# Query and key tiles of the plain heads: transposed in 32x32 blocks by VectorE, and five shared DRAM tiles in the second expert layer

## The chip, the cores and the metric

The kernel runs on one core of one Trainium2 chip. The metric is the device time of one execution in microseconds; several runs are taken and their median is given. The engines are called as in the profile: PE (TensorE matmul), PEld (its weight load), DVE (VectorE), ACT (ScalarE), POOL (GpSimd) and SP (SyncE, which here only issues transfers; "SPq" are its DMA instructions).

## The reference, in short

Three stages follow each other. The first is windowed attention with 4 batches, 8 heads, 576 positions and a head width of 64. Heads 0 to 3 are plain (each position sees itself and the 31 before it), heads 4 to 7 are dilated (it sees every fourth position of the last 128):

```
scores = (1 / sqrt(64)) * q @ k^T
scores = where(mask of the head, scores, -1e9)
attn   = exp(scores - max);  attn /= sum(attn) + 1e-9
x      = attn @ v                     # 2304 rows of 512
```

Then come two mixture-of-experts layers over the 2304 rows, each with 8 experts of 512 -> 1024 -> 512. The first takes the best expert of each row that a skip score lets through; the second adds a noise term to the logits and takes the best two experts.

## The kernel before, in words

**Attention.** The work is cut into 16 units of two heads of one batch. Units 0, 1, 6, 7, 10, 11, 14 and 15 hold dilated heads; units 2, 3, 4, 5, 8, 9, 12 and 13, eight in all, hold plain ones. A unit passes these steps:

- `load_qk` (L91): SP issues the transfers of q and k into the tiles `qld` and `kld`, three buffers each. A dilated tensor is one transfer (L99). A plain tensor is two, one for each head (L103), each 96 partitions x 6 x 64 floats, so 576 packets of 256 bytes.
- `qk_T` (L138), called step A: PE transposes q and k against an identity (L146), three blocks of 96 x 96 to a PSUM bank, four banks to a unit (q twice, k twice), which is 12 instructions. DVE evicts each bank: k with a copy (L158), q with a multiplication by -0.125 (L160). `qT` and `kT` exist four times.
- `scores`, step B: PE multiplies (L175), in a first part of five query blocks and a second of four. For each block DVE adds the mask and takes the minimum (L178, two instructions in the trace: the pass, and a short read of the accumulator), ACT takes the exponential and its sum (L182), DVE the reciprocal of the sum for the whole part (L184, L185, tile `rs`), and POOL multiplies (L186). The score carries a minus sign, which the factor in L160 puts in.
- `probs_T` (L197), step D: PE transposes the probabilities, ACT (L202) and DVE (L200) evict. `values` (L214, L232), step E: PE multiplies by v.

**What sets the order.** The order on PE is written out by hand: in the plan of a step (L948), A belongs to unit s + 1, B to unit s, D and E to earlier units: "A0 D0 A1 B0 A2 D1 B1 A3 X E X D2", where X is a piece of the later rows and routing work. The order on DVE, ACT, POOL and SP is chosen by a scheduler when the program is built. Right behind the last A of a unit, `ahead` issues the loads of the unit three later, once its buffers are free. The v tile comes next in SP's queue: for the first unit 13 transfers (L132).

**After attention** come the first expert layer (first matmul L741) and the second (L439 to L441). In the second layer, `put` (L1260) writes the gathered rows of an expert to a DRAM tile `xq`, `spread` (L1267) reads that tile back in four transfers, 32 partitions each, and `turn_v` (L1287) has DVE transpose the 32x32 blocks (L1294), reading with a stride and writing with a stride. There are 35 tiles `xq`, one for each expert and each of five row tiles.

Of the kernel before, what the change touches and what calls it, by code (L numbers as in the profile page):

```python
# [8 lines left out]
F32 = mybir.dt.float32  # L9
# [3 lines left out]
ALU = mybir.AluOpType  # L13
AF = mybir.ActivationFunctionType
# [4 lines left out]
BIG = 1.0e9  # L19


def dram(ap, offset, dims):
    return bass.AP(tensor=ap.tensor, offset=ap.offset + offset, ap=dims)


class Attention:
# [7 lines left out]
    def __init__(self, ctx, early, tc, bank, q, k, v, ident, xT):  # L34
        self.tc, self.nc, self.bank = tc, tc.nc, bank
        self.q, self.k, self.v = q, k, v
        self.ident, self.xT = ident, xT
        self.B, self.H, self.S, self.D = q.shape
        nc = self.nc
        self.NB = self.S // 64  # L40

        self.vp = ctx.enter_context(tc.tile_pool(name="at_v", bufs=2))
        self.wk = ctx.enter_context(tc.tile_pool(name="at_wk", bufs=2))
        fix = early.enter_context(tc.tile_pool(name="at_fix", bufs=1, side="right"))
        self.ld = early.enter_context(tc.tile_pool(name="at_ld", bufs=2, side="right"))
        NB, R = self.NB, self.S // 4


        ip = fix.tile([128, 1], I32, name="ip")
        nc.gpsimd.iota(ip, pattern=[[0, 1]], base=0, channel_multiplier=1)  # L50
        nc.vector.tensor_single_scalar(ip, ip, 63, op=ALU.bitwise_and)
        fi = fix.tile([128, 2], F32, name="fi")
        nc.vector.tensor_copy(fi[:, 0:1], ip)
        nc.vector.tensor_scalar(fi[:, 1:2], fi[:, 0:1], 32.0, None, op0=ALU.add)
        col = fix.tile([128, 96], F32, name="col")
        nc.gpsimd.iota(col, pattern=[[1, 96]], base=0, channel_multiplier=0, allow_small_or_imprecise_dtypes=True)
        inner = fix.tile([128, 96], F32, name="mask_in")
        nc.vector.tensor_scalar(inner, col, fi[:, 0:1], BIG, op0=ALU.is_le, op1=ALU.mult)
        nc.vector.tensor_scalar(col, col, fi[:, 1:2], BIG, op0=ALU.is_gt, op1=ALU.mult)
        nc.vector.tensor_max(inner, inner, col)  # L60
        first = fix.tile([128, 96], F32, name="mask_first")
        nc.vector.tensor_copy(first, inner)
        nc.vector.memset(first[:, :32], BIG)
        self.mask = [[first] + [inner] * (NB - 1), [first] + [inner] * (NB - 1)]
        rowbig = fix.tile([128, 1], F32, name="rowbig")
        for n in range(1, NB):
            for b in range(R, self.S, R):
                i0, c0 = b - 64 * n, b - 64 * n + 32
                if c0 <= 0 or i0 >= 64:
                    continue  # L70
                m = fix.tile([128, 96], F32, name=f"mask_{n}")
                nc.gpsimd.tensor_copy(m, inner)
                nc.vector.tensor_scalar(rowbig, fi[:, 0:1], float(i0), BIG, op0=ALU.is_ge, op1=ALU.mult)
                nc.vector.tensor_scalar(m[:, :min(c0, 96)], m[:, :min(c0, 96)], rowbig, None, op0=ALU.max)
                self.mask[1][n] = m
        self.kT, self.qT = [], []
        for i in range(4):
            t = fix.tile([128, 32 + self.S], F32, name=f"kT{i}")
            nc.vector.memset(t[:, :32], 0.0)
            self.kT.append(t)  # L80
            self.qT.append(fix.tile([128, self.S], F32, name=f"qT{i}"))
        self.tiles, self.vt, self.pT, self.p = {}, {}, {}, {}
# [7 lines left out]

    def load_qk(self, m):  # L91

        nc = self.nc
        b, hp, dil = self.unit(m)
        base = (b * self.H + 2 * hp) * self.S * 64
        for nm, src in (("q", self.q), ("k", self.k)):
            if dil:
                t = self.ld.tile([96, 6, 128], F32, name=f"{nm}ld", bufs=3)
                nc.sync.dma_start(t, dram(src, base, [[128, 96], [192 * 64, 6], [1, 128]]))  # L99
            else:  # L100
                t = self.ld.tile([96, 6, 2, 64], F32, name=f"{nm}ld", bufs=3)
                for h in range(2):
                    nc.sync.dma_start(t[:, :, h, :], dram(src, base + h * self.S * 64, [[64, 96], [96 * 64, 6], [1, 64]]))  # L103
                t = t.rearrange("p c h d -> p c (h d)")
            self.tiles[nm, m] = t

    def load_v(self, m):
# [30 lines left out]
    def qk_T(self, m, part):  # L138

        nc = self.nc  # L140
        b, hp, dil = self.unit(m)
        nm, g = "qk"[part // 2], part % 2
        src = self.tiles[nm, m]
        pt = self.bank("tp")[:, :288].rearrange("p (c a) -> p c a", c=3)
        for c in range(3):
            nc.tensor.transpose(pt[:, c, :], src[:, 3 * g + c, :], self.ident[:96, :96])  # L146
        t = self.kT[m % 4][:, 32:] if nm == "k" else self.qT[m % 4]
        if dil:
            o = t.rearrange("p (h s c a) -> p h s c a", h=2, s=2, c=3)[:, g]
            i_ = pt.rearrange("p c (a s) -> p s c a", s=2)  # L150
        else:
            o = t[:, 288 * g:288 * g + 288]
            i_ = pt.rearrange("p c a -> p (c a)")
        scale = 1.0 if nm == "k" else -0.125
        if m < 2 and g == 1:
            nc.scalar.activation(o, i_, AF.Copy, scale=scale)
        elif nm == "k":
            nc.vector.tensor_copy(o, i_)  # L158
        else:
            nc.vector.tensor_scalar(o, i_, scale, None, op0=ALU.mult)  # L160

    def scores(self, m, part):
        nc, NB = self.nc, self.NB
        b, hp, dil = self.unit(m)
# [11 lines left out]
                                 start=True, stop=True)  # L176
        for n in range(n0, n1):
            nc.vector.tensor_tensor_reduce(out=sm[:, n, :], in0=ps[:, n - n0, :], in1=self.mask[dil][n],  # L178
                                           scale=1.0, scalar=3.0e38, op0=ALU.add, op1=ALU.min,
                                           accum_out=nmax[:, n:n + 1])  # L180
        for n in range(n0, n1):
            nc.scalar.activation(sm[:, n, :], sm[:, n, :], AF.Exp, bias=nmax[:, n:n + 1], scale=-1.0,  # L182
# [4 lines left out]
                                in1=rs[:, n0:n1, None].to_broadcast([128, n1 - n0, 96]), op=ALU.mult)  # L187
# [332 lines left out]
def tile_attention_moe_moe(ctx, tc, q, k, v, w_skip, w_gate, w1, w2, v_gate, v_noise, noise, u1, u2, out):  # L520
    nc = tc.nc
    B, H, S, D = q.shape
    N, DM = B * S, H * D
# [30 lines left out]
    dr = ctx.enter_context(tc.tile_pool(name="dr", bufs=1, space=DRAM))  # L554
# [131 lines left out]
    for op, *t in steps:  # L686
        if t and op[0] in "hpHP":
            c = ORDER[int(t[0])]
# [265 lines left out]
    m = (128 * LT + N) // 2  # L954
    early_ = [lambda: logits_l(128 * LT, m), lambda: logits_l(m, N)] + late(rows_l, 0, 2) + [lambda: write_l(0, 256), logits_Tl]
    busy(24)
    for n in range(-LA, NU + LE):
        a, s, d, e = n + LA, n + LB, n, n - LE
        for op in plan[n].split():
            i = int(op[1]) if len(op) > 1 else 0  # L960
# [255 lines left out]
    with ExitStack() as lctx:  # L1216
# [41 lines left out]
        xT2, xq = {}, {}  # L1258

        def put(e, i):  # L1260

            if e < E:
                n = rows2[i]
                xq[e, i] = dr.tile([n, DM], F32, name=f"xq{e}_{i}")
                nc.sync.dma_start(xq[e, i], X.pop((e, i))[:n])

        def spread(e, i):  # L1267
# [418 lines left out]
```

## Time and profile before

| | |
|---|---|
| median of the runs shown | 787.04 us (787.05, 781.78, 787.04) |
| profiled execution | 781.75 us, of it 779.9 us span |
| mean granted clock of TensorE | 0.984 of full speed |
| PE busy | 738.9 us, 95% of the span |
| DVE, ACT, POOL busy | 391.0, 309.7, 267.2 us |
| first matmul of the first expert layer (L741) | 133.7 us |

How to read it: the time of an execution is its span (first to last instruction of the core) and 1.85 us around it. An engine that is busy 95% of the span is likely to carry the chain that ends last, but within attention, the first 130 us, the engines hand work to each other every microsecond, so each stretch has to be read by itself. In the rows further down, a time in front is counted from the start of the span, "x20" is a number of instructions, and what stands behind "<-" in brackets is what ended the engine's idle time. Granted clock 1.00 is the higher of TensorE's two levels.

### The profile page before, as it was taken

How to read it: one execution, taken by the hardware profiler on the slowest of the kernel's cores; microseconds unless marked ns; L12 is line 12 of the kernel's file. 1: busy time of each engine (PE TensorE's matmuls, PEld its weight loads, DVE VectorE, ACT ScalarE, POOL GpSimd, SP SyncE). 2: the span in 40 equal slices, each digit the busy share in tenths (PEclk: the TensorE clock that was granted, in tenths of full speed). 3: DMA queues.
4: the chain of work that ended last, by engine and by line, in shares of the span. 5: the costliest groups of instructions: out<-in, count | busy, mean ns of one | idle time of the engine just before them, and what ended most of it. 6: DMA issues, size and time to landing. Idle time of an engine off the chain costs nothing.

```text
span 779.9 us, 14489 instructions
## 1 busy us (share of the span) xinstructions
PE 738.9 (95%) x5428; PEld 627.5 (80%) x5428; DVE 391.0 (50%) x1242; ACT 309.7 (40%) x824; POOL 267.2 (34%) x251
## 2 busy tenths in 40 slices
PE   8999989899998999898999899999999999999994
PEld 7877768676875977787797797898997988988883
DVE  7866866728218529936644337444453552240110
ACT  5887852234225253223442433442442433332120
POOL 3322210225127133155525434523322424544011
PEclk9999989999999999999999999999999999999997
DMA  7979555597889896268898788717417445323112
GB/s 182 174 173 251 128 203 188 179 354 265 287 264 313 301 329 242 69 171 216 237 304 236 185 262 239 170 56 159 132 64 160 121 139 92 115 29 46 15 25 29
DMA packets 133420, 138.54 MB, mean 178 GB/s; under 512 B 45184, under 2 KB 85248, under 8 KB 133344
## 3 DMA queue, kind: packets, MB, share of 16 engines
q1 hardware_dynamic: 122224, 113.39, 47.1%
q0 software_dynamic: 9808, 22.86, 14.8%
q10 hardware_dynamic: 1312, 1.31, 0.5%
q8 instruction: 44, 0.72, 0.4%
q14 instruction: 32, 0.26, 0.1%
HBM read 105.22 MB, written 32.31 MB: 176 GB/s over the span
## 4 chain that ended last, share of the span: by engine, by line
PE 65%; DMA 11%; DVE 10%; issue 5%; ACT 4%; POOL 3%; SPq 1%; POOLq 0%; DVEq 0%; ACTq 0%
PE pt L439 8%; PE pt L441 8%; PE pt L440 8%; PE pt L749 5%; PE s L741 4%; DMA xg<-xs,gidx 4%; PE s L439 3%; PE po L441 3%; PE s L440 3%; PE s L441 3%; PE po L439 3%; PE po L440 3%; ACT sm L182 3%; DMA xq<-xg 3%; PE s L175 2%
## 5 line engine op out<-in xcount | busy, mean ns | idle before, releaser
L434 POOL TENSOR_TENSOR wlo<-wraw,whi 128x512 fp32r<-128x512 f32 x76 | 109.7, 1500 | 145.0 <-ACT whi L433 120.6
L439 PE MATMUL pt<-whi,hh 128*128 128x512 f32 (+1 forms) x320 | 127.7, 399 | 3.9 <-ACT y L1450 3.9
L440 PE MATMUL pt<-wlo,hh 128*128 128x512 f32 (+1 forms) x320 | 126.6, 396 | 0.0
L441 PE MATMUL pt<-whi,hl 128*128 128x512 f32 (+1 forms) x320 | 126.6, 396 | 0.0
L434 DVE TENSOR_TENSOR wlo<-wraw,whi 128x512 fp32r<-128x512 f32 x84 | 83.9, 1010 | 85.1 <-ACT whi L433 78.3
L433 ACT ACTIVATE whi<-wraw 128x512 fp32r<-128x512 f32 x160 | 91.1, 622 | 56.9 <-PE po L440 17.1
L1210 POOL DMA_INDIRECT out_dram<-y,sidx x40 | 63.0, 1575 | 123.1 <-ACT y L1450 120.4
L713 POOL DMA_INDIRECT xg<-xs,gidx x51 | 51.1, 1002 | 132.1 <-DMA xq<-xg 45.3
L439 PEld LDWEIGHTS pt<-whi,hh 128*128 128x128 f32 (+1 forms) x320 | 58.7, 184 | 20.2 <-ACT y L1450 5.2
L439 PE MATMUL s<-xh,whi 128*128 128x256 f32 (+1 forms) x256 | 72.5, 283 | 1.3 <-DVE hl L1436 1.3
L441 PE MATMUL s<-xh,wlo 128*128 128x256 f32 (+1 forms) x256 | 72.5, 283 | 0.0
L441 PE MATMUL po<-xh,wlo 128*128 128x352 f32 x224 | 72.5, 324 | 0.0
L439 PE MATMUL po<-xh,whi 128*128 128x352 f32 x224 | 72.5, 324 | 0.0
L440 PE MATMUL s<-xl,whi 128*128 128x256 f32 (+1 forms) x256 | 72.4, 283 | 0.0
L440 PE MATMUL po<-xl,whi 128*128 128x352 f32 x224 | 72.2, 322 | 0.0
L441 PEld LDWEIGHTS pt<-whi,hl 128*128 128x128 f32 (+1 forms) x320 | 58.8, 184 | 15.9
L440 PEld LDWEIGHTS pt<-wlo,hh 128*128 128x128 f32 (+1 forms) x320 | 58.9, 184 | 15.3 <-issue 0.2
L1436 DVE SCALAR_TENSOR_TENSOR hl<-po,hh 128x352 fp32r<-128x352 f32 x56 | 29.2, 522 | 71.1 <-ACT hh L1435 69.4
L1450 ACT ACTIVATE y<-pt,slots 128x512 f32<-128x512 f32 (+1 forms) x40 | 27.3, 682 | 88.0 <-PE pt L441 68.0
L182 ACT ACTIVATE sm<-sm,nmax 128x96 f32<-128x96 f32 x144 | 51.9, 362 | 18.6 <-DVE nmax L178 18.2
L1436 DVE SCALAR_TENSOR_TENSOR hl<-s,hh 128x256 fp32r<-128x256 f32 (+1 forms) x64 | 27.3, 427 | 57.2 <-ACT hh L1435 52.5
L186 POOL TENSOR_TENSOR sm<-sm,rs 128x480 f32<-128x480 f32 (+1 forms) x32 | 29.1, 910 | 78.3 <-DVE nmax L178 52.2
(407 smaller groups left out, 1468.8 us busy)
## 6 DMA issues: line engine op xcount, KB each, us to landing
wraw<-in_moe_w_dram SPq DMA_DIRECT2D x40, 1024.0 KB
whi<-in_moe_w_dram SPq DMA_DIRECT2D x12, 1024.0 KB
wlo<-in_moe_w_dram SPq DMA_DIRECT2D x12, 1024.0 KB
xq<-xg SPq DMA_DIRECT2D x28, 256.0 KB
xs<-xq SPq DMA_DIRECT2D x112, 64.0 KB
out_dram<-zt SPq DMA_DIRECT2D x46, 128.0 KB
xs<-xr SPq DMA_DIRECT2D x13, 256.0 KB
v<-in_v_dram SPq DMA_DIRECT2D x7, 432.0 KB
```

Of the source, the lines that this page charges most:

```text
L182: nc.scalar.activation(sm[:, n, :], sm[:, n, :], AF.Exp, bias=nmax[:, n:n + 1], scale=-1.0, accum_out=ssum[:, n:n + 1])
L186: nc.gpsimd.tensor_tensor(out=sm[:, n0:n1, :], in0=sm[:, n0:n1, :], in1=rs[:, n0:n1, None].to_broadcast([128, n1 - n0, 96]), op=ALU.mult)
L433: nc.scalar.activation(hi, src, AF.Copy)
L434: (eng or nc.vector).tensor_tensor(out=lo, in0=src, in1=hi.bitcast(F32), op=ALU.subtract)
L439: nc.tensor.matmul(out, lhsT=a[0], rhs=b[0], start=start, stop=False)
L440: nc.tensor.matmul(out, lhsT=a[0], rhs=b[1], start=False, stop=False)
L441: nc.tensor.matmul(out, lhsT=a[1], rhs=b[0], start=False, stop=stop)
L713: gather.last = nc.gpsimd.indirect_dma_start(out=xg, out_offset=None, in_=xs[:n, :], in_offset=bass.IndirectOffsetOnAxis(ap=idx, axis=0))
L741: nc.tensor.matmul(ph[:, 128 * f:128 * f + 128], lhsT=w[:, c, 128 * f:128 * f + 128], rhs=self.x[:, c], start=c == 0, stop=c == KC - 1)
L749: nc.tensor.matmul(self.py, lhsT=self.h[:, 4 * g + f], rhs=w[:, f], start=g == 0 and f == 0, stop=g == 1 and f == 3)
L1210: s = nc.gpsimd.indirect_dma_start(out=out, out_offset=bass.IndirectOffsetOnAxis(ap=idx, axis=0), in_=y, in_offset=None, compute_op=ALU.add)
L1436: nc.vector.scalar_tensor_tensor(hl[1][:, f, s_], in0=ph, scalar=0.0, in1=hl[0][:, f, s_].bitcast(F32), op0=ALU.max, op1=ALU.subtract)
```

## The change

For plain units `load_qk` brings q and k in as [128, 576]: four transfers to a tensor instead of two, each 32 partitions x 18 x 32 floats, so 576 packets of 128 bytes each. Partition 32h + a then holds, for half a head h, row a of each group of 32 positions. `qk_T` makes the whole transposed tensor of a plain unit with one DVE instruction that transposes 32x32 blocks (128 x 576), without PE and PSUM. Dilated units are transposed by PE as before. The factor -0.125 moves from the eviction into the masked minimum (its `scale` operand), and the masks are multiplied by -8 to match. The 35 DRAM tiles `xq` of the second layer become five, one for each row tile, that the experts use in turn. Lines behind the edit shift by one or two: scores L174, minimum L177, exponential L181, reciprocal L183 and L184, transposing probabilities L196.

```diff
     def load_qk(self, m):
         for nm, src in (("q", self.q), ("k", self.k)):
+            t = self.ld.tile([128, 768], F32, name=f"{nm}ld", bufs=3)
             if dil:
-                t = self.ld.tile([96, 6, 128], F32, name=f"{nm}ld", bufs=3)
+                t = t[:96].rearrange("p (c d) -> p c d", c=6)
                 nc.sync.dma_start(t, dram(src, base, [[128, 96], [192 * 64, 6], [1, 128]]))
             else:
-                t = self.ld.tile([96, 6, 2, 64], F32, name=f"{nm}ld", bufs=3)
-                for h in range(2):
-                    nc.sync.dma_start(t[:, :, h, :], dram(src, base + h * self.S * 64, [[64, 96], [96 * 64, 6], [1, 64]]))
-                t = t.rearrange("p c h d -> p c (h d)")
+                t = t[:, :576].rearrange("p (g d) -> p g d", d=32)
+                for h in range(4):
+                    nc.sync.dma_start(t[32 * h:32 * h + 32], dram(src, base + (h // 2) * self.S * 64 + (h % 2) * 32,
+                                                                  [[64, 32], [32 * 64, self.S // 32], [1, 32]]))
...
     def qk_T(self, m, part):
+        t = self.kT[m % 4][:, 32:] if nm == "k" else self.qT[m % 4]
+        if not dil:
+            if g == 0:
+                nc.vector.transpose(out=t, in_=src.rearrange("p g d -> p (g d)"))
+            return
...
-        scale = 1.0 if nm == "k" else -0.125
...
-            nc.vector.tensor_scalar(o, i_, scale, None, op0=ALU.mult)
...
     def scores(self, m, part):
-                                           scale=1.0, scalar=3.0e38, op0=ALU.add, op1=ALU.min,
+                                           scale=-0.125, scalar=3.0e38, op0=ALU.add, op1=ALU.min,
...
         def put(e, i):
-                xq[e, i] = dr.tile([n, DM], F32, name=f"xq{e}_{i}")
+                xq[e, i] = dr.tile([n, DM], F32, name=f"xq{i}")
```

How the order moves, at the place where unit 4 follows unit 3. Unit 4 has the tiles `kT_192` and `qT_194`, unit 5 `kT_195` and `qT_197`; the row with `mask_first` is the first minimum of unit 4. On DVE before, the last reciprocal of unit 3 stands among the q evictions of unit 5:

```order
L158 COPY kT_192<-tp 128x288
L160 TENSOR_SCALAR qT_197<-tp 128x288
L184 TENSOR_SCALAR rs<-ssum 128x4
L160 TENSOR_SCALAR qT_197<-tp 128x288
L185 RECIPROCAL rs<-rs 128x4
L178 ISA sm,nmax<-s,mask_first 128x96
```

On DVE of the changed kernel:

```order
L183 TENSOR_SCALAR rs<-ssum 128x4
L184 RECIPROCAL rs<-rs 128x4
L149 STREAM_TRANSPOSE qT_194<-qld 128x576
L149 STREAM_TRANSPOSE kT_192<-kld 128x576
L177 ISA sm,nmax<-s,mask_first 128x96
```

Before, what stands behind the reciprocal's first half makes a tile of unit 5; now both transposes behind the reciprocal make the tiles of unit 4 itself, whose scores the next row reads.

On PE, the scores of unit 4, before:

```order
L146 MATMUL tp<-ident,qld 128x96 x3
L197 MATMUL pt<-ident,sm 96x128 x3
L146 MATMUL tp<-ident,qld 128x96 x3
L175 MATMUL s<-kT_192,qT_194 64x96 x10
L146 MATMUL tp<-ident,kld 128x96 x3
L197 MATMUL pt<-ident,sm 96x128 x3
L175 MATMUL s<-kT_192,qT_194 64x96 x8
L146 MATMUL tp<-ident,kld 128x96 x3
```

and in the changed kernel:

```order
L231 MATMUL po_613<-pT,v_391 64x64
L196 MATMUL pt<-ident,sm 96x128 x6
L174 MATMUL s<-kT_192,qT_194 64x96 x10
L196 MATMUL pt<-ident,sm 96x128 x3
L174 MATMUL s<-kT_192,qT_194 64x96 x8
L231 MATMUL po_714<-pT,v_391 64x64
```

The four groups of L146, which made unit 5's tiles, are gone from around the scores; what is left of PE's order is as it was. At units 3 and 5 the DVE rows stand in the same way; at units 2, 8, 9 and 12 one of the two transposes stands behind the last sum (L183) of the unit ahead and the other earlier, at unit 13 both stand behind it.

## Rows read from the trace of the kernel before

**Rows 1.** Windows of 20 us in attention: busy time (and count) of each engine
```profile
core 0: us, PE busy (x) PEld busy (x) DVE busy (x) ACT busy (x) POOL busy (x), PEclk, DMA share, GB/s
20.00:40.00 20.00, 19.38 (x326) 16.65 (x326) 15.79 (x103) 18.28 (x84) 7.06 (x9) 1.00 0.87 167
60.00:80.00 20.00, 18.20 (x291) 14.19 (x290) 12.87 (x80) 14.87 (x61) 4.53 (x7) 1.00 0.94 232
```

**Rows 2.** Timeline of PE: first scores of units 2 to 5, 8, 12, 13
```profile
18.39 1.04 PE L175 MATMUL s<-kT,qT 64*64 64x96 f32 x20
...
23.30 1.04 PE L175 MATMUL s<-kT,qT 64*64 64x96 f32 x20
...
26.20 1.39 PE L232 MATMUL po<-pT,v 96*64 96x64 f32 x40
...
28.81 1.04 PE L175 MATMUL s<-kT,qT 64*64 64x96 f32 x20
...
34.32 1.04 PE L175 MATMUL s<-kT,qT 64*64 64x96 f32 x20
...
46.98 1.04 PE L175 MATMUL s<-kT,qT 64*64 64x96 f32 x20
54.06 1.04 PE L175 MATMUL s<-kT,qT 64*64 64x96 f32 x20
...
75.79 1.04 PE L175 MATMUL s<-kT,qT 64*64 64x96 f32 x20
82.92 1.04 PE L175 MATMUL s<-kT,qT 64*64 64x96 f32 x20
89.66 1.04 PE L175 MATMUL s<-kT,qT 64*64 64x96 f32 x20
```

**Rows 3.** Chain of waits from 28 to 36 us: start, duration, what
```profile
29.85 0.40 PE tp L146 x3
...
34.14 0.25 PE tp L146 x3
```

**Rows 4.** Timeline of ACT: exponentials, first and last of unit 4, first of 5
```profile
30.31 0.38 ACT L182 ACTIVATE sm<-sm,nmax 128x96 f32<-128x96 f32 x1
...
33.34 0.36 ACT L182 ACTIVATE sm<-sm,nmax 128x96 f32<-128x96 f32 x1
...
36.04 0.37 ACT L182 ACTIVATE sm<-sm,nmax 128x96 f32<-128x96 f32 x1 [0.45 <-DVE nmax L178]
```

**Rows 5.** Timeline of DVE between unit 4 and unit 5
```profile
34.14 0.18 DVE L185 RECIPROCAL rs<-rs 128x4 f32<-128x4 f32 x1
34.24 0.79 DVE L160 TENSOR_SCALAR qT<-tp 128x288 f32<-128x288 f32 x2
35.52 0.26 DVE L178 CUSTOM_DVE_ANT_0 sm<-s,mask_first 128x96 f32<-128x96 f32 x1 [0.49 <-PE s L175]
```

**Rows 6.** Groups by line, shapes apart, DVE: count, busy us, mean ns
```profile
L1294 DVE STREAM_TRANSPOSE xt<-xs 128x512 f32<-128x512 f32 x28 | 30.8, 1098 | 21.9 <-DMA xs<-xq 21.2
...
L160 DVE TENSOR_SCALAR qT<-tp 128x288 f32<-128x288 f32 x30 | 13.3, 451 | 10.2 <-PE tp L146 9.7
...
L812 DVE COPY xr<-tp 128x512 f32<-128x512 f32 x9 | 6.2, 684 | 1.3 <-PE tp L807 1.3
...
L1294 DVE STREAM_TRANSPOSE xt<-xs 128x384 f32<-128x384 f32 x7 | 6.0, 863 | 5.2 <-DMA xs<-xq 5.0
```

**Rows 7.** Tile qld: issues on SP, ns min/median/max; then timeline of SP
```profile
L103 SPq DMA_DIRECT2D qld<-in_q_dram x16: 384/508/2976, 2.8 to 64.3; - x16
...
13.52 7.07 SPq L132 DMA_DIRECT2D v<-in_v_dram x13
```

**Rows 8.** Transfers in 7 to 9 us (256-byte packets), in 25 to 28 us (32-byte)
```profile
DMA packets 2131, 0.53 MB, mean 266 GB/s; under 512 B 2131, under 2 KB 2131, under 8 KB 2131
...
DMA packets 3508, 0.11 MB, mean 36 GB/s; under 512 B 3508, under 2 KB 3508, under 8 KB 3508
```

**Rows 9.** Windows of 5 us (columns as in the first group)
```profile
100.00:105.00 5.00, 4.21 (x65) 3.69 (x65) 4.74 (x34) 2.65 (x13) 0.46 (x1) 0.75 0.37 104
105.00:110.00 5.00, 5.00 (x42) 4.20 (x38) 1.74 (x12) 2.91 (x12) 1.36 (x2) 0.57 0.34 97
```

More of the change, by code (lines that the diff above doesn't have):

```diff
@@ L57, in __init__ @@
         inner = fix.tile([128, 96], F32, name="mask_in")
-        nc.vector.tensor_scalar(inner, col, fi[:, 0:1], BIG, op0=ALU.is_le, op1=ALU.mult)
-        nc.vector.tensor_scalar(col, col, fi[:, 1:2], BIG, op0=ALU.is_gt, op1=ALU.mult)
-        nc.vector.tensor_max(inner, inner, col)
+        nc.vector.tensor_scalar(inner, col, fi[:, 0:1], -8 * BIG, op0=ALU.is_le, op1=ALU.mult)
+        nc.vector.tensor_scalar(col, col, fi[:, 1:2], -8 * BIG, op0=ALU.is_gt, op1=ALU.mult)
+        nc.vector.tensor_tensor(out=inner, in0=inner, in1=col, op=ALU.min)
         first = fix.tile([128, 96], F32, name="mask_first")
         nc.vector.tensor_copy(first, inner)
-        nc.vector.memset(first[:, :32], BIG)
+        nc.vector.memset(first[:, :32], -8 * BIG)
         self.mask = [[first] + [inner] * (NB - 1), [first] + [inner] * (NB - 1)]
@@ L72, in __init__ @@
                 nc.gpsimd.tensor_copy(m, inner)
-                nc.vector.tensor_scalar(rowbig, fi[:, 0:1], float(i0), BIG, op0=ALU.is_ge, op1=ALU.mult)
-                nc.vector.tensor_scalar(m[:, :min(c0, 96)], m[:, :min(c0, 96)], rowbig, None, op0=ALU.max)
+                nc.vector.tensor_scalar(rowbig, fi[:, 0:1], float(i0), -8 * BIG, op0=ALU.is_ge, op1=ALU.mult)
+                nc.vector.tensor_scalar(m[:, :min(c0, 96)], m[:, :min(c0, 96)], rowbig, None, op0=ALU.min)
                 self.mask[1][n] = m
@@ L146, in qk_T @@
             nc.tensor.transpose(pt[:, c, :], src[:, 3 * g + c, :], self.ident[:96, :96])
[L147 to L150, printed above, removed]
-        else:
-            o = t[:, 288 * g:288 * g + 288]
-            i_ = pt.rearrange("p c a -> p (c a)")
-        scale = 1.0 if nm == "k" else -0.125
-        if m < 2 and g == 1:
-            nc.scalar.activation(o, i_, AF.Copy, scale=scale)
-        elif nm == "k":
+        o = t.rearrange("p (h s c a) -> p h s c a", h=2, s=2, c=3)[:, g]
+        i_ = pt.rearrange("p c (a s) -> p s c a", s=2)
+        if m < 2 and g == 1:
+            nc.scalar.activation(o, i_, AF.Copy)
+        else:
             nc.vector.tensor_copy(o, i_)
-        else:
-            nc.vector.tensor_scalar(o, i_, scale, None, op0=ALU.mult)
     def scores(self, m, part):
```

## The prediction, made before the changed kernel ran

> **What bounds the kernel now.** I read the busy times by window first, then the chain of waits in the stretch that the edit touches, then the timelines of the engines on that chain. In the windows of attention the reader is to see that PE is busy 19.38 of 20 us from 20 to 40 us, with ACT at 18.28 and DVE at 15.79, all at full granted clock [rows 1]: PE sets the pace, and ACT is close behind. The chain of waits from 28 to 36 us agrees: it stays on PE, and between the scores of unit 4 and those of unit 5 it holds four groups of the transposes that the change removes, two of 0.40 us and two of 0.25 us, 1.30 us together [rows 3]. From first scores to first scores, unit 2 to 3 takes 4.91 us, 3 to 4 takes 5.51, 4 to 5 takes 5.51 [rows 2]. The timelines of ACT and DVE show the second loop, nearly as long: scores of unit 4 start at 28.81, its first exponential at 30.31, its last at 33.34, ending 33.70; the last reciprocal follows at 34.14, and DVE is free for the next thing at 34.24 [rows 2, 4, 5]. Before, PE does not wait for this loop: unit 5's scores start at 34.32, because its tiles were made a unit earlier, and DVE's first minimum waits for PE until 35.52 [rows 2, 5].
>
> **The change, part by part.**
>
> *Removed on PE.* 1.30 us on the chain for each plain unit, eight of them: 10.4 us if PE stayed the bound everywhere. That is the most the change can give.
>
> *Removed on DVE.* Four evictions of 0.45 us [rows 6] a unit; two run in 0.79 us [rows 5], so some 1.6 us. The multiplication by -0.125 costs nothing where it went: the minimum is the same pass with another constant. The masks are built once, by as many instructions.
>
> *Added on DVE.* Two transposes of 128 x 576. The trace has the same operation at 128 x 512 in 1.098 us and at 128 x 384 in 0.863 us, thus 1.84 ns a column [rows 6]; at 576 that gives 1.22 us, the upper end, since those read and write with strides. The lower end is a plain pass: 0.684 us for 512 columns and 0.451 for 288, thus 1.04 ns a column and 0.75 us for 576 [rows 6]. The new ones are contiguous on both sides, like the plain passes, so I take d = 0.8 us and keep both ends. [...]
>
> *Moved on DVE, and the wait that it adds.* This is the step that decides. The rows of the order show both transposes of units 3, 4 and 5 behind the last reciprocal of the unit ahead, and PE's scores need them. So PE now waits for the second loop. Unit 5's scores would start at 34.24 + 2d + 0.1 for the hand-over (an estimate: 34.24 less the 34.14 of the step before it), that is at 34.34 + 2d instead of 34.32 [rows 2, 5]. From scores to scores this is 28.81 to 34.34 + 2d, 5.53 + 2d; the k evictions no longer stand among the minima, which can take back 0.15 us, since nine exponentials at 0.36 us are 3.24 us and ran in 3.39 [rows 4]. With d = 0.8 a period is 7.0 us. Behind the waiting scores on PE stand the next probability transposes and values, which are late with them, and ACT waits for the scores through the minimum. Three such periods are 21.0 us in place of 15.93 (18.39 to 34.32 [rows 2]): +5.1 us. The PE relief there buys nothing; PE is simply idle while DVE transposes.
>
> *Unit 2* has one transpose in that place: 5.4 + 0.8 = 6.2 us. Against the 4.91 and 5.51 us of the units behind it [rows 2] this is 0.7 to 1.3 more, and the unit ahead of it, whose period held unit 2's PE transposes, can be up to 1.30 us shorter [rows 3]. Between -0.6 and +1.3 I take +0.5.
>
> *Units 8, 9, 12, 13.* Here X pieces lengthen the periods: unit 7 to 8 takes 7.08 us, 12 from 11 takes 7.13, 13 from 12 takes 6.74 [rows 2]. PE alone could save 1.30 in each. One transpose in the loop gives 6.2 us, which is below 7.1, so units 8 and 12 may gain 0.9 each and 9 a little; two, at unit 13, give 7.0, a loss of 0.3. That is -1.8 at best; PE is busy 18.20 of 20 us there and DVE also carries row work [rows 1], so I take -1 and keep -1.8 to 0.
>
> *Loads.* 32 more transfers, each 0.51 us of SP by the median [rows 7]: 16 us of SP in all. Twelve of them come ahead of the first v, whose 13 issues begin at 13.52 and take 7.07 us [rows 7]; 6 us later they would end near 26.6, where PE multiplies by v at 26.20 [rows 2]. I take +1 us for that (0 to 2). In packets, the first three plain units have 6,912 of 256 bytes, at 2131 in 2 us [rows 8] 6.5 us; now 13,824 of 128 bytes: 13.0 us at the same price each, or 11.8 us at the pace of the 32-byte packets, 3508 in 3 us [rows 8]. The transposes come almost a unit later than the PE ones did, so most of this is hidden; it is cover that would be gone in the second rival.
>
> *Shared xq tiles.* A put must wait until the spread of the expert before has read its tile. The names of SP's waits and the order of its rows in the second layer are as before, and the puts stand behind those reads on the same queue. Nothing.
>
> *Sum.* 5.1 + 0.5 - 1 + 1 = 5.6, say +5.5 us at the end of attention. What follows is PE's chain with the same order, so it passes through. Against the profiled execution: 781.75 + 5.5 = 787.3 us. That execution lies with the lower of the three runs; two of three are 5.3 us higher, and I assume the changed kernel has the same two levels: 787.04 + 5.5 = **792.5, say 792 us**. With d at its ends the four places (two transposes at units 3, 4, 5 and 13) move the sum by -0.4 and +3.4.
>
> **The rivals.**
>
> *The relief of PE wins.* If the transposes are cheap or the exponentials end early enough, units stay bound by PE, and 1.30 us goes from each of eight: -10.4 us, 776.6 us; -5 if half do. For it: PE is 97% busy from 20 to 40 us. Against it: the order on DVE, and ACT at 18.28 of 20 [rows 1]. It decides from a period below 5.5 us, which needs 2d near 0.
>
> *Loads late and transposes slow.* With d = 1.22 the sum is +9. If the loads also reach the transposes late, early units wait for the queue: 13.0 us less 6.5 is 6.5 us at most for the first three, and I count half. Together +9 to +13: 796 to 800 us. For it: SP and the queues are busy from the start, DMA share 0.87 [rows 1]. It decides once a 128-byte packet costs as much as one of 256. [...]
>
> *The clock falls in the new waits.* From 100 to 105 us PE is busy 4.21 of 5 us with DVE at 4.74, and the granted clock is 0.75, in the next 5 us 0.57, between its two levels [rows 9]; ten us of PE work at that mean of 0.66 lose 3.4 us. New idle of 1.6 us a unit from 20 to 45 us can bring one such fall there: 792.5 + 3.4 = 796 us. If instead the new order avoids the old fall, 789 us.
>
> **How the numbers follow.** A measurement of this kernel can tell about 1%, 7.9 us, from no change: below 779.2 is faster, above 794.9 slower. Chances: the forecast, +1 to +7.9 us, 0.45; loads and slow transposes 0.24; the clock 0.12; the relief of PE 0.19, nearly all of it below 779. So faster 0.17, same 0.46, slower 0.37. The range: low end 778, where most of the relief comes, high end 804, the second rival with one clock fall; the forecast's own range is 786 to 797 by the two levels of the runs and the ends of d.
>
> **What would show it.** In the changed profile: transposes near 0.8 us (1.2 would mean the upper end); from 20 to 45 us PE's busy time falls by 2 to 4 us in 20 and its scores wait for DVE's transposes at units 3, 4 and 5; those periods are near 7.0 us; the first matmul of the expert layer stands near 139 us instead of 133.7; the rest of the program keeps its length. The prediction is wrong if the periods stay at 5.5 us or below, if the scores wait for loads and not for transposes that have started, or if the later units give back more than 2 us.

## The result, and the profile after

Twenty runs of each kernel give a median of 787.10 us (781.63 to 789.88) after the change and 783.47 us (776.28 to 788.44) before it. The ratio of the runs is **1.0063, 95% interval 1.0042 to 1.0084**: slower by 4.9 us of 783.47. The two medians by themselves lie 3.6 us apart, a ratio of 1.0046, inside the interval. So the change is slower, clear of noise, by less than 1%. The profiled execution after has a span of 784.6 us against 779.9, and the first matmul of the first expert layer stands at 139.84 us against 133.56 (timeline of PE; the table ahead has 133.7, from the chain of waits).

The window of 20 to 40 us (columns as in [rows 1]) shows where to look:

```profile
20.00:40.00 20.00, 13.87 (x195) 11.15 (x193) 12.55 (x75) 14.14 (x63) 5.76 (x7) 0.81 0.60 115
60.00:80.00 20.00, 18.95 (x301) 15.20 (x301) 14.71 (x80) 15.91 (x68) 5.62 (x7) 1.00 0.74 168
```

PE lost 5.5 us of busy time in the first of them, more than the work that left it (nine groups of three transposes, at most 0.47 us each, 4 us), and no other engine took its place as a busy one: from 20 to 40 us the core waits. The timeline of PE, which answers to [rows 2], says for what. These are the first scores of units 2 to 6 and, between them, the first transposes of the dilated unit 6:

```profile
18.24 1.87 PE L174 MATMUL s<-kT,qT 64*64 64x96 f32 x20 [3.82 <-DVE rs L184]
26.27 1.04 PE L174 MATMUL s<-kT,qT 64*64 64x96 f32 x20 [2.44 <-DVE kT L149]
33.19 1.04 PE L174 MATMUL s<-kT,qT 64*64 64x96 f32 x20 [1.00 <-DVE kT L149]
39.98 0.47 PE L153 MATMUL tp<-ident,qld 96*128 96x96 f32 x3 [2.69 <-DMA qld<-in_q_dram]
40.95 1.62 PE L174 MATMUL s<-kT,qT 64*64 64x96 f32 x20
47.90 1.04 PE L174 MATMUL s<-kT,qT 64*64 64x96 f32 x20
```

Before, PE waited for nothing at these scores. Now those of units 3 and 4 wait for the k transpose, and ahead of unit 5's PE stands for 2.69 us before a load. Unit 2's wait for DVE too, for 3.82 us, and yet start no later than before (18.24 against 18.39), with no transposes to do on PE ahead of them. The periods are 8.03, 6.92 and 7.76 us (forecast 7.0 each, before 4.91, 5.51, 5.51). The timeline of DVE at the start of unit 4, which answers to [rows 5], is the gap as forecast:

```profile
31.52 0.18 DVE L184 RECIPROCAL rs<-rs 128x4 f32<-128x4 f32 x1
31.70 0.78 DVE L149 STREAM_TRANSPOSE qT<-qld 128x576 f32<-128x576 f32 x1
32.40 0.73 DVE L149 STREAM_TRANSPOSE kT<-kld 128x576 f32<-128x576 f32 x1
...
34.39 0.26 DVE L177 CUSTOM_DVE_ANT_0 sm<-s,mask_first 128x96 f32<-128x96 f32 x1 [1.25 <-PE s L174]
```

Last reciprocal, two transposes, then DVE itself waits 1.25 us for the scores that waited for it. One transpose takes 0.78 us and the next starts 0.70 us after it; the group has 8 for q and 8 for k (by line, DVE, as in [rows 6]):

```profile
L149 DVE STREAM_TRANSPOSE qT<-qld 128x576 f32<-128x576 f32 x8 | 6.2, 778 | 0.4 <-issue 0.4
L149 DVE STREAM_TRANSPOSE kT<-kld 128x576 f32<-128x576 f32 x8 | 6.1, 762 | 0.4 <-DMA v<-in_v_dram 0.4
```

The timeline of SP, which answers to [rows 7], shows the second thing, the issues of v for the first unit at 19.10 instead of 13.52, and unit 5's q behind them at 26.26 (before: 20.70):

```profile
17.00 2.06 SPq L105 DMA_DIRECT2D kld<-in_k_dram  x4
19.10 7.05 SPq L134 DMA_DIRECT2D v<-in_v_dram  x13
26.26 3.16 SPq L105 DMA_DIRECT2D qld<-in_q_dram  x4
```

A third thing is the clock. By windows of the changed kernel, the column before the last two is the granted clock:

```profile
18.00:24.00 6.00, 5.59 (x45) 4.34 (x45) 2.57 (x23) 3.17 (x17) 1.28 (x2) 0.50 0.60 127
...
28.00:32.00 4.00, 4.00 (x62) 3.65 (x60) 2.51 (x18) 3.90 (x20) 1.14 (x2) 0.62 0.59 95
32.00:40.00 8.00, 4.32 (x85) 3.38 (x83) 5.11 (x27) 5.71 (x24) 2.80 (x4) 1.00 0.70 112
40.00:45.00 5.00, 5.00 (x51) 4.19 (x51) 3.25 (x15) 2.39 (x11) 0.00 (x0) 0.66 1.20 237
```

After PE had stood still for 3.82 us ahead of 18.24 the granted clock is 0.50, the lower level, for 6 us, where it had been 1.00 before the change.

So the profile after holds three suspects for the same 20 us: transposes in the gap, loads that come late, and the clock. The trace alone can't part them, since an engine's idle time is put down to whichever came last.

### The profile page after: what moved, and what is told of

Read it like the earlier page. It is cut to its first block, busy times and chain, and to the rows that moved or that the text cites. A ratio compares the mean times of both kernels' runs of the same rounds, so it can differ in the third digit from the quotient of the medians.

```text
span 784.6 us, 14333 instructions
## 1 busy us (share of the span) xinstructions
PE 735.6 (94%) x5332; PEld 622.6 (79%) x5332; DVE 393.0 (50%) x1226; ACT 308.6 (39%) x824; POOL 268.0 (34%) x251
## 2 busy tenths in 40 slices
DMA packets 152364, 138.54 MB, mean 177 GB/s; under 512 B 64128, under 2 KB 104192, under 8 KB 152288
## 4 chain that ended last, share of the span: by engine, by line
PE 66%; DMA 13%; DVE 8%; ACT 4%; issue 3%; SPq 3%; POOL 2%; POOLq 0%; DVEq 0%; ACTq 0%
PE pt L438 9%; PE pt L440 8%; PE pt L439 8%; PE s L740 5%; PE po L440 4%; PE po L438 4%; PE po L439 4%; PE s L438 4%; PE s L439 4%; PE s L440 4%; PE pt L748 4%; ACT sm L181 2%; DMA xg<-xs,gidx 2%; PE s L174 2%; DMA qld<-in_q_dram 2%
## 5 line engine op out<-in xcount | busy, mean ns | idle before, releaser
L433 DVE TENSOR_TENSOR wlo<-wraw,whi 128x512 fp32r<-128x512 f32 x84 | 85.6, 1030 | 89.3 <-ACT whi L432 79.7
L440 PEld LDWEIGHTS pt<-whi,hl 128*128 128x128 f32 (+1 forms) x320 | 59.0, 184 | 15.9
L181 ACT ACTIVATE sm<-sm,nmax 128x96 f32<-128x96 f32 x144 | 51.8, 361 | 23.9 <-DVE nmax L177 23.7
```

The source lines that it names most:

```text
L433: (eng or nc.vector).tensor_tensor(out=lo, in0=src, in1=hi.bitcast(F32), op=ALU.subtract)
L440: nc.tensor.matmul(out, lhsT=a[1], rhs=b[0], start=False, stop=stop)
```

## The experiments

In all tables and sentences, "k on POOL" means that POOL instead of SP issues the k loads of plain units. The first scores of the units and the start of the expert layer come from each kernel's one profiled execution, the ratio from 6 or 12 runs against runs of the kernel before (20 of each for the change itself; early2_cheap ran once):

| kernel | scores of unit 2 | 3 | 4 | 5 | 6 | expert layer | ratio to before (95%) |
|---|---|---|---|---|---|---|---|
| before | 18.39 | 23.30 | 28.81 | 34.32 | 39.71 | 133.56 | 1 |
| the change | 18.24 | 26.27 | 33.19 | 40.95 | 47.90 | 139.84 | 1.0063 (1.0042 to 1.0084) |
| xq_only | 17.94 | 22.84 | 28.35 | 33.86 | 39.26 | 133.04 | 0.9998 (0.9970 to 1.0025) |
| loads128 | 18.02 | 22.92 | 32.30 | 40.10 | 45.49 | 140.15 | 1.0066 (1.0042 to 1.0091) |
| early2 | 17.18 | 23.78 | 32.45 | 41.97 | 48.17 | 139.16 | 1.0028 (0.9997 to 1.0059) |
| cheap_late | 19.81 | 27.70 | 35.56 | 42.84 | 48.23 | 132.22 | not comparable |
| early2_cheap | 19.27 | 23.29 | 28.99 | 34.51 | 39.90 | 125.13 | not comparable |
| late_pool | 14.68 | 23.39 | 31.42 | 38.52 | 45.47 | 134.65 | 0.9950 (0.9916 to 0.9984) |
| early2_pool | 14.64 | 20.62 | 26.03 | 32.41 | 38.91 | 131.03 | 0.9940 (0.9910 to 0.9969) |
| before_pool | 17.86 | 22.91 | 28.42 | 33.93 | 39.32 | 126.13 | 0.9898 (0.9858 to 0.9939) |
| dbl | 20.59 | 29.19 | 37.78 | 46.55 | 53.48 | 150.44 | 1.0206 (1.0158 to 1.0255) |
| clock | 18.46 | 25.78 | 32.42 | 40.00 | 45.39 | 135.46 | 1.0060 (1.0033 to 1.0087) |
| mixed_early2 | 16.59 | 21.49 | 27.01 | 32.52 | 38.03 | 130.77 | 0.9960 (0.9925 to 0.9995) |
| mixed_pool | 18.26 | 23.29 | 28.81 | 34.32 | 39.71 | 130.34 | 0.9969 (0.9935 to 1.0003) |

The theory at the start was the one of the prediction, the gap; the first rival was that the loads cost, the second that the clock does.

**The shared tiles alone (xq_only).** Before, with one line of the change:

```diff
-                xq[e, i] = dr.tile([n, DM], F32, name=f"xq{e}_{i}")
+                xq[e, i] = dr.tile([n, DM], F32, name=f"xq{i}")
```

> The kernel before with one part of the change alone: the five shared DRAM tiles of the second layer, attention untouched. Theory (the cost of the change comes from the transposes that wait in the gap between two units): no difference, a ratio to before of 1.000 within 0.002. Rival (the shared tiles add a wait between the write of one expert's rows and the reads of the expert before): up to the whole 1.006.

Measured 0.9998, no difference within some 2 us. So the cost is looked for in attention.

**The loads alone (loads128).** Before, with four transfers of 128-byte packets, still transposed by PE:

```diff
-                    nc.sync.dma_start(t[:, :, h, :], dram(src, base + h * self.S * 64, [[64, 96], [96 * 64, 6], [1, 64]]))
+                    for j in (0, 32):
+                        nc.sync.dma_start(t[:, :, h, j:j + 32], dram(src, base + h * self.S * 64 + j, [[64, 96], [96 * 64, 6], [1, 32]]))
```

> The kernel before with the loads of the plain units cut as in the change: four transfers to a tensor, 576 packets of 128 bytes each, but still 96 partitions and transposed by PE. Theory (gap): the loads alone cost 0 to 2 us, ratio 1.000 to 1.003, since PE then waits for some of them at units 3 to 5 only. Rival (the loads are the price: twice the issues on SP and twice the packets): 1.006 or more, with PE waiting for qld and kld by 5 us or more in the first 45 us.

Measured 1.0066: as much as the whole change, and the theory's 0 to 2 us is missed. The rival holds by its ratio, though the waits below sum to 3.6 us and not to 5. Every wait of PE for a transfer from 17 to 49 us in its timeline, with first scores of units 3 to 5 among them:

```profile
22.92 1.04 PE L176 MATMUL s<-kT,qT 64*64 64x96 f32 x20
27.51 0.31 PE L233 MATMUL po<-pT,v 96*64 96x64 f32 x4 [0.79 <-DMA v<-in_v_dram]
28.41 0.91 PE L233 MATMUL po<-pT,v 96*64 96x64 f32 x22 [0.59 <-DMA v<-in_v_dram]
30.54 0.71 PE L147 MATMUL tp<-ident,qld 96*128 96x96 f32 x3 [0.76 <-DMA qld<-in_q_dram]
32.30 1.68 PE L176 MATMUL s<-kT,qT 64*64 64x96 f32 x20
39.15 0.44 PE L147 MATMUL tp<-ident,qld 96*128 96x96 f32 x3 [1.47 <-DMA qld<-in_q_dram]
40.10 1.04 PE L176 MATMUL s<-kT,qT 64*64 64x96 f32 x20
```

The reader sees v first, then the loads behind v in SP's queue. In this kernel SP begins v at 19.21, in the change at 19.10: the delay is that of 12 more issues at about 0.5 us. These transfers to 96 partitions are as late as those to 32 partitions in the change, and cost as much (1.0066 against 1.0063); a transfer to 32 partitions by itself was not tried.

**The order alone (early2).** The change, with the last reciprocal of a unit, and the sum ahead of it, held behind both transposes of the next:

```diff
...
+        with self.tc.issue_after(self.turned[m + 1]) if part and m + 1 in self.turned else nullcontext():
-        nc.vector.tensor_scalar(rs[:, n0:n1], ssum[:, n0:n1], 1.0e-9, None, op0=ALU.add)
+            nc.vector.tensor_scalar(rs[:, n0:n1], ssum[:, n0:n1], 1.0e-9, None, op0=ALU.add)
```

> The changed kernel with one edit of DVE's order: the second reciprocal of a unit must stand behind both transposes of the next plain unit, so that these run while ACT still takes the last four exponentials. Theory (gap): the periods from scores to scores at units 3, 4, 5 fall from 8.0, 6.9 and 7.8 us to about 6.0 and the ratio to before goes from 1.006 to 0.997 to 1.001 (4 to 7 us less than the changed kernel). Rival (late loads): the transposes wait for their data in the new place, periods stay near 7 us, ratio 1.004 to 1.008. Rival (clock): the granted clock below 1.00 goes only if the waits go.

Measured 1.0028, between the ranges of the theory and of the rival; its interval overlaps the change's. Unit 6 starts at 48.17, no earlier than in the change: at units 4 and 5 the gap is empty, at unit 3 a wait of 1.02 us is left, and the time is gone all the same. DVE makes unit 4's tiles by 28.92, and then (timeline of DVE, then of PE)

```profile
27.49 0.78 DVE L149 STREAM_TRANSPOSE qT<-qld 128x576 f32<-128x576 f32 x1
28.19 0.73 DVE L149 STREAM_TRANSPOSE kT<-kld 128x576 f32<-128x576 f32 x1
...
34.12 0.26 DVE L177 CUSTOM_DVE_ANT_0 sm<-s,mask_first 128x96 f32<-128x96 f32 x1 [4.92 <-PE s L174]
```

```profile
28.21 0.34 PE L232 MATMUL po<-pT,v 96*64 96x64 f32 x4 [1.62 <-DMA v<-in_v_dram]
29.00 0.31 PE L232 MATMUL po<-pT,v 96*64 96x64 f32 x4 [0.45 <-DMA v<-in_v_dram]
29.74 1.33 PE L232 MATMUL po<-pT,v 96*64 96x64 f32 x22 [0.44 <-DMA v<-in_v_dram]
32.45 1.50 PE L174 MATMUL s<-kT,qT 64*64 64x96 f32 x20
40.20 0.72 PE L153 MATMUL tp<-ident,qld 96*128 96x96 f32 x3 [3.19 <-DMA qld<-in_q_dram]
```

PE waits 2.5 us in the middle of the values for v and 3.19 us for unit 6's q. In the change the first is not there and the second is 2.69 us: the gap had already made PE late. The theory of one chain falls; a theory of two chains side by side takes its place.

**Cheap loads, first with the transposes in the gap, then without (cheap_late, early2_cheap).** Two kernels that compute attention on shuffled positions: q and k of a plain unit come as one contiguous transfer to a tensor. Other rows are routed behind it, so only the time to the expert layer counts.

```diff
-                for h in range(4):
-                    nc.sync.dma_start(t[32 * h:32 * h + 32], dram(...))
+                nc.sync.dma_start(t.rearrange("p g d -> p (g d)"), dram(src, base, [[576, 128], [1, 576]]))
```

The first of them also queues the transposes of units 3, 4, 5 and 13 behind the last reciprocal of the unit ahead, the second has the edit of the kernel above.

> The changed kernel with q and k of plain units brought in by one contiguous transfer to a tensor (128 packets of 2304 bytes), which puts the numbers in another arrangement, so that attention is computed on shuffled positions; the transposes of units 3, 4, 5 and 13 are held behind the last reciprocal of the unit ahead, as in the changed kernel. Theory (gap): periods at units 3 to 5 stay at 6.9 us or above, ratio 1.003 to 1.006; the late load of unit 6 goes (2.7 us of PE idle, of which some 0.3 us count). Rival (late loads): 1.000 or below.

> Both suspects taken away: the contiguous loads that shuffle positions, and the second reciprocal held behind the transposes. Only the time up to the first matmul of the expert layer counts, since other rows are routed behind it. Theory (two chains): periods at units 3 to 5 of 5.0 to 6.0 us and a start of the expert layer at 125 to 130 us, against 133.6 before, 139.8 in the change and 132.2 with cheap loads and transposes in the gap. Rival (only the loads cost): about 132. Rival (only the gap costs): about the same as the order alone gave with the real loads, 139.

In the first, units 3 to 5 keep periods of 7.89, 7.86 and 7.28 us (from the scores of unit 2 at 19.81 to those of unit 5 at 42.84), so the gap costs by itself; yet the expert layer starts at 132.22. In the second the periods are 4.02, 5.70, 5.52 and the expert layer starts at 125.13. Neither part alone gives that: with the order alone (early2) it starts at 139.16.

**k on POOL (early2_pool, late_pool).** One word in the loads of the change, with the order of the kernel above and, in the second kernel, with the transposes held in the gap:

```diff
-                    nc.sync.dma_start(t[32 * h:32 * h + 32], dram(...))
+                    (nc.gpsimd if nm == 'k' else nc.sync).dma_start(t[32 * h:32 * h + 32], dram(...))
```

This word does two things. POOL issues the k loads, and their packets come out larger: the kernel moves the same 138.54 MB with 18,432 fewer packets under 512 bytes, as many as the k loads of plain units have in the change, and 1,024 more from there to 8 KB. The packets of the whole kernel (from the pages) are, in the change, in early2_pool and in the kernel before:

```profile
DMA packets 152364, 138.54 MB, mean 177 GB/s; under 512 B 64128, under 2 KB 104192, under 8 KB 152288
DMA packets 134956, 138.54 MB, mean 180 GB/s; under 512 B 45696, under 2 KB 86272, under 8 KB 134880
DMA packets 133420, 138.54 MB, mean 178 GB/s; under 512 B 45184, under 2 KB 85248, under 8 KB 133344
```

With k on POOL the small packets are nearly as few as before the change (45,696 under 512 bytes against 45,184). So these kernels take away late loads, but don't tell fewer issues on SP from fewer packets, as the rival in the first of the two expectations here asks.

> The reordered changed kernel with the k loads of plain units issued by POOL, so that SP has as many issues as before the change and the data is the right one. Theory (two chains): the waits for v at 27 to 30 us and for unit 6's qld at 40 us go, ratio 0.992 to 0.999. Rival (packets, not issues, are what is late): the waits stay, ratio 1.002 to 1.006. Rival (POOL's issues hold up its own multiplications): the second transposes of probabilities are late, ratio above 1.003.

> The changed kernel with the k loads of plain units issued by POOL (right data, SP relieved), but the transposes of units 3, 4, 5 and 13 held behind the last reciprocal of the unit ahead, as in the changed kernel. Theory (the gap costs by itself): periods at units 3 to 5 stay at 6.9 us or more, ratio 1.003 to 1.007. Rival (the late loads are the whole cost): as the other kernel with k on POOL, 0.994.

With both cures the ratio is 0.9940, inside the theory's range, and no scores from 17 to 40 us wait:

```profile
20.62 1.04 PE L174 MATMUL s<-kT,qT 64*64 64x96 f32 x20
26.03 1.04 PE L174 MATMUL s<-kT,qT 64*64 64x96 f32 x20
32.41 1.04 PE L174 MATMUL s<-kT,qT 64*64 64x96 f32 x20
38.91 1.04 PE L174 MATMUL s<-kT,qT 64*64 64x96 f32 x20
```

With the gap put back and the loads relieved:

```profile
23.39 1.86 PE L179 MATMUL s<-kT,qT 64*64 64x96 f32 x20 [3.45 <-DVE kT L152]
31.42 1.04 PE L179 MATMUL s<-kT,qT 64*64 64x96 f32 x20 [1.38 <-DVE kT L152]
38.52 1.80 PE L179 MATMUL s<-kT,qT 64*64 64x96 f32 x20 [2.18 <-DVE kT L152]
```

Both start unit 2 at 14.6 to 14.7 and unit 6 at 38.91 and 45.47: **the gap by itself is 6.6 us at unit 6**, 6.1 of them between the scores of units 2 and 5 (23.84 us against 17.77). At the expert layer 3.6 of it are left, and in the runs the two can't be told apart (0.9940, 0.9950): the expectation of 1.003 to 1.007 is missed, and its rival, 0.994, lies inside the interval. So the gap's cost is shown in the profiles, and not in the time of the whole. Whether the scheduler would close the gap without the edit once the loads are on POOL, no run here shows; that moving the loads changes the order that it gives DVE is seen in the control, which follows.

**The control: k on POOL in the kernel before (before_pool).** The same word, in the loads of the kernel before.

> A control: the kernel before with the k loads of plain units issued by POOL, transposes on PE as they were. Theory (SP had slack before, the gain of the last kernel with k on POOL comes from the transposes that left PE): ratio 0.998 to 1.002. Rival (the gain is SP's relief alone): 0.993 to 0.996.

0.9898, the best of the kernels that can be compared, and beyond both expectations. So the gain of 0.9940 above is not the transposes'. Little of it comes from the first 45 us (unit 6 at 39.32 against 39.71): 1.7 us are there at unit 14 (95.98 against 97.70), 6.1 at unit 15 and 7.4 at the expert layer, so most of it comes at 100 us. In the kernel before, DVE had put pieces of routing ahead of the q evictions of unit 15, and the granted clock fell behind the wait of 2.05 us, to 0.75 and 0.57 in windows of 5 us [rows 9]:

```profile
100.80 0.47 PE L146 MATMUL tp<-ident,kld 96*128 96x96 f32 x3 [2.05 <-DVE qT L160]
```

In the control the scheduler puts these evictions ahead of much of the routing, PE doesn't wait for them, and the same windows read

```profile
100.00:105.00 5.00, 4.82 (x85) 4.00 (x83) 5.00 (x22) 3.47 (x13) 1.84 (x2) 1.00 0.43 118
105.00:110.00 5.00, 4.45 (x73) 3.34 (x70) 4.46 (x33) 4.41 (x21) 0.99 (x1) 1.00 0.57 175
```

Unit 15's scores start at 101.44 instead of 107.54, and the expert layer at 126.13 instead of 133.56. This cause is read from the two traces; no run moved the evictions alone.

**Transposes twice (dbl).**

```diff
+                for _ in range(2):
-                nc.vector.transpose(out=t, in_=src.rearrange("p g d -> p (g d)"))
+                    nc.vector.transpose(out=t, in_=src.rearrange("p g d -> p (g d)"))
```

> The changed kernel with each of the 16 transposes done twice (0.70 us more each). Theory (gap chain alone sets the pace at units 3, 4, 5 and 13): two more transposes in each of four gaps, 5.6 us, and part of 0.7 at units 2, 8, 9 and 12: ratio to before 1.013 to 1.017. Theory (late loads run beside it, nearly as long): at unit 5 and behind it part is hidden, ratio 1.009 to 1.013. Rival (only the loads cost): 1.006 to 1.008.

1.0206, above all the ranges: 11.2 us more than the change, if the ratios are taken times 783.47, with some 4 us of uncertainty either way. Sixteen transposes of 0.70 us are 11.2 us, but by the profiles not all of them count. The expert layer starts 10.6 us later than in the change, and 1.0 of that is there at the first scores of unit 0 already (8.88 against 7.84). From the scores of unit 2 to those of unit 5 six more transposes, 4.2 us, add 3.3 (25.96 against 22.71); in this kernel the scheduler puts one q transpose of units 3 and 4 ahead of the last sum. From unit 6 to the expert layer 5.0 of 5.6 us arrive, so those that were forecast to be half hidden mostly count. At unit 5 no wait for a load is left (timeline of PE), the gap has taken its place:

```profile
46.55 1.04 PE L175 MATMUL s<-kT,qT 64*64 64x96 f32 x20 [3.85 <-DVE kT L150]
```

**The clock (clock).** The change, with small matmuls that nobody reads where PE waits ahead of units 2 to 5:

```diff
+    for s_, k in ((2, 28), (3, 16), (4, 8)):
+        plan[s_ - LB] = plan[s_ - LB].replace("B0", f"Y{k} B0")
+    plan[5 - LB] = "Y16 " + plan[5 - LB]
```

> The changed kernel with small matmuls that nobody reads (28, 16, 8 and 16 of 128 columns, some 0.1 us each) where PE waits ahead of the scores of units 2 to 5. Theory (the clock that fell in the new waits is part of the price): the granted clock stays at 1.00 from 16 to 45 us, unit 3's period falls from 8.0 to about 7.0 us and unit 5's from 7.8 to 7.2, ratio 1.003 to 1.005. Rival (the slow stretches lie beside the two chains and cost nothing): ratio 1.006. Rival (the fillers run into the scores): 1.008 or more.

The clock mostly holds (windows of this kernel; the change had 0.50, 0.62 and 0.66):

```profile
18.00:24.00 6.00, 5.51 (x61) 4.51 (x61) 2.97 (x24) 3.66 (x19) 1.77 (x2) 0.72 0.50 121
...
28.00:32.00 4.00, 2.64 (x58) 2.37 (x54) 2.71 (x15) 4.00 (x18) 1.82 (x2) 1.00 0.79 121
...
40.00:45.00 5.00, 5.00 (x91) 4.40 (x91) 3.75 (x26) 3.56 (x17) 0.96 (x1) 1.00 1.31 232
```

In the profile unit 6 comes 2.5 us earlier than in the change and the expert layer 4.4 us, but the ratio is 1.0060, the same as the change's. In that profile one price can be seen: from unit 5 to unit 6 it is 5.39 us with the granted clock at 1.00, as before the change, and 6.95 in the change, at 0.66. What the fallen clock costs the whole is not settled; in the runs the fillers gave nothing back, as the first rival said.

**The change where PE is the bound (mixed_early2, mixed_pool).** Units 2 to 5 as before, units 8, 9, 12 and 13 by DVE, first with all loads on SP, then with k on POOL:

```diff
...
-        if not dil:
+        if not dil and m >= 6:
             if g == 0:
...
```

> The change for units 8, 9, 12 and 13 only, with the second reciprocal of the unit ahead held behind their transposes; units 2 to 5 load and transpose as in the kernel before. Theory (two chains of nearly equal length in the first 45 us, the transposes in the gap and the late loads; later units have slack on SP and are bound by PE): the early periods stay at 4.9, 5.5 and 5.5 us, each of the four later units gets up to 1.3 us shorter, ratio 0.995 to 0.999. Rival (late loads at any place): PE waits for qld or v between 45 and 90 us, ratio 1.000 to 1.004.

> Transposes by DVE for units 8, 9, 12 and 13 only, and the k loads of all plain units issued by POOL. Theory (the transposes by DVE give something where PE is the bound, units 8 to 13, and cost where ACT's loop is): ratio to before 0.984 to 0.989, below the 0.990 of the control with k on POOL and all transposes on PE. Rival (the gain of these kernels is the order that the scheduler makes when it takes the loads to be early, and the transposes by DVE give nothing): 0.990 to 0.994.

0.9960 and 0.9969: the first lies in the theory's range, the second above both of its ranges. But in the first the four units give nothing: from the scores of unit 6 to those of unit 13 it takes 50.1 us against 50.0 before, and 1.7 us are there at unit 6 already, where units 2 to 5 still load and transpose as before. With k on POOL the same stretch takes 48.6 us against 49.1 in the control, half a microsecond less, while the ratio of the control (0.9898) is the better one; the two intervals overlap only at 0.9935 to 0.9939. So no kernel here shows, in its runs, a gain that the transposes by DVE would bring over the same loads with PE.

## Why the prediction was right, and which step was not

*The direction and the size.* Forecast +5.5 us, a ratio of 1.007 on the 787.04 us shown; 792 stands to that as 1.0063. Measured 1.0063. That the time itself, 787.10, lies 4.9 us below 792 is mostly the base: the runs shown then had two levels by chance, and twenty runs spread from 776 to 788 with the median 3.6 us lower; the rest is that the medians rose by 3.6 us and not by 5. The assumption of two levels was wrong.

*The duration.* Taken 0.8, measured 0.778 and 0.762, and 0.70 from start to start. The contiguous form is thus near the 0.75 us estimated from the plain pass for 576 columns [rows 6]; with one shape the trace can't part the pace from a fixed cost. The strided form of the second layer took 1.098 us for fewer columns [rows 6]. The nearest row was the plain pass, not the row with the same name. The minimum with `mask_first` took 0.253 us with the factor in it, 0.255 before (by line, mean of 16 each).

*The wait.* Scores wait for the transposes at units 3 and 4 as forecast. At unit 5 two things end almost together: PE stands before unit 6's q until 39.98, DVE's second transpose ends at 40.64, and the scores start at 40.95. The three periods are 22.7 us together, forecast 21.0, before 15.9. So the step held in kind. PE's busy time from 20 to 40 us fell by 5.5 us, not by the 2 to 4 forecast.

*The step that failed* is the one on the loads: "6 us later they would end near 26.6 ... I take +1 us for that". Alone they cost 1.0066, as much as the whole change. SP's 12 more issues were counted and the delay of v was right to half a microsecond (forecast 6, measured 5.6); what was missed is how many things stand behind v on the same queue: unit 5's q and k, and then unit 6's, for which PE waits in its fixed order (0.76 and 1.47 us with the loads alone, 2.69 in the change).

*The sum* added the two. They lie side by side. Four kernels with the transposes on DVE cross them, by the start of unit 6: neither 38.91 (early2_pool), the gap alone 45.47 (late_pool), the loads alone 48.17 (early2), both 47.90 (the change). Alone they cost 6.6 and 9.3 us, together 9.0. (Some of the 9.3 is lost ahead of unit 2, which starts at 17.18 instead of 14.64.) Two wrong things met: the loads were too cheap in the sum, and the sum should have been nearer to a maximum. The right total is partly luck. At unit 6 the change is 8.2 us behind the kernel before, where the terms up to there made 6.6.

*The later relief* of 1 us: units 6 to 14 took 58.2 us against 58.0, so it was not there. What did come back lies behind unit 14: from there to unit 15 it is 6.05 us in the change (106.13 to 112.18) and was 9.84 before [rows 9]. PE's wait for unit 15's evictions is 0.52 us there instead of 2.05, and the granted clock from 105 to 110 us is 1.00 instead of 0.57. The prediction had that only as the 789 us of a rival. The clock does fall elsewhere, to 0.73 from 100 to 105 us, behind a wait of 1.56 us for a transpose of unit 13.

```profile
106.13 1.04 PE L174 MATMUL s<-kT,qT 64*64 64x96 f32 x20
112.18 1.04 PE L174 MATMUL s<-kT,qT 64*64 64x96 f32 x20
```

```profile
100.00:105.00 5.00, 5.00 (x73) 4.36 (x74) 4.16 (x22) 3.94 (x18) 1.66 (x2) 0.73 1.23 261
105.00:110.00 5.00, 4.48 (x70) 3.73 (x70) 4.97 (x36) 2.57 (x10) 0.17 (x1) 1.00 0.75 195
```

So the units from 6 to 15 gave back 3.6 us, more than the 2 us that the prediction named as a sign of being wrong; from unit 15 to the expert layer 1.6 us were lost again.

*The rest of the program* was to pass the delay through. 6.3 us at the expert layer became 4.9 in the runs. By profiled executions the time from there to the end of the span runs from 637.1 us (k on POOL, early) to 649.2 us (the control), so a single execution prices a change of a few us badly, and whether a delay at the expert layer passes through in full stays open; the ratios above carry the verdicts.

*Rivals.* The shared tiles: nothing, as said. The relief of PE: did not come, not even with the gap and the late loads both gone. In early2_pool the periods of units 3 to 6 are 5.98, 5.41, 6.38 and 6.50 us, before they were 4.91, 5.51, 5.51 and 5.39: PE waits there for the evictions of the probabilities, as in

```profile
28.53 0.53 PE L197 MATMUL pt<-ident,sm 128*96 128x128 f32 x3 [1.46 <-ACT pT L202]
```

Loads late and transposes slow: the loads were late, beside the gap instead of on top of it, and the transposes were not slow (0.778 and 0.762 us). The clock: it fell as described, to 0.50, 0.62 and 0.66 in the windows above, and its price stays open.

## What to carry to other kernels

Before you take work off the busiest engine, ask what its inputs and outputs now wait for: here two 0.7 us transposes stand in a loop that had been nearly as long as PE's, and most of their time counted. When a load is cut into more transfers, add up the issues ahead of everything that stands behind it on its queue, not only what the load itself feeds. Two delays over the same stretch need not add (here 6.6 and 9.3 us came to 9.0), and taking away one of them may show little; cross the two in four kernels, and run the cure on the kernel before as a control, where it may be worth more than the change.

## What was not expected of the hardware

Half the bytes are not half the issue: SP takes 2.06 us for four transfers of 72 KB, about 0.5 us each, as it took about 0.5 us for one of 144 KB [rows 7]. It is no fixed price: the first four of a plain tensor in the change took 4.57 us, with the DMA engines 0.99 busy from 5 to 8 us. Whether the twice as many issues or the twice as many packets make the loads late, no run parts. For the issues speaks that in the change SP issues almost without a pause from 9.7 to 26 us, while the DMA engines are 0.67 busy over that time. In the control POOL issues one of the k loads in 0.76 us (16 in 12.1 us), and PE waits for no transfer from 7 to 50 us. And the granted clock fell to 0.50 for 6 us behind one wait of 3.82 us.
